# RWKV-like recurrence with an MLP mixer on one core: old state added on VectorE instead of TensorE from chunk 32 on, with a new order

## The chip, the cores and the metric

One core of a Trainium2 chip. The metric is the device time of one execution in microseconds, from several runs of each kernel; the median counts. Beside it stands one profiled execution, from which all rows of the trace come.

Engines: PE is TensorE (matmuls; its weight loads are a row of their own, PEld), DVE is VectorE, ACT is ScalarE, POOL is GpSimd, SP issues most of the DMAs. Each works through its own queue in order.

## What is computed

For each of 4 batch elements and 8 heads a state of 40 x 40 runs over 768 steps; its readings become the input of a token MLP and a channel MLP with residuals:

```
for t in range(S):                       # B=4, H=8, S=768, D=40
    y[:, :, t] = einsum('bhd,bhde->bhe', rt, state)
    Sa = einsum('bhde,bhe->bhd', state, at)
    state = state * wt[:, :, None, :] - einsum('bhd,bhe->bhde', Sa, bt) + einsum('bhd,bhe->bhde', vt, kt)
x = y as (B, S, 320)
u = x + (relu(x^T @ w_tok1) @ w_tok2)^T      # 768 -> 256 -> 768
out = u + relu(u @ w_ch1) @ w_ch2            # 320 -> 1536 -> 320
```

## The kernel before

The recurrence is done in chunks of 64 steps: 12 chunks for each batch element, 48 in all, numbered g. For each pair of chunks `t_a` and `t_b`/`t_b2` prepare matrices that don't depend on the state (cumulative products of w, products of k, b and a, and the inverse of a triangular matrix, which `t_solve` finds on VectorE for eight chunks at a time). `t_chain` then runs the chunks one behind the other, in two halves (`gi`) of four heads. One step `body(g)` of a half is:

- `pq` (L1165), a copy to the state buffer `Gb` on ScalarE (L1172), `pr2` (L1191): products with the old state; ScalarE negates the results into `W2s` (L1228, L1230), and the masks of L1200, L1216 and L1217 go on POOL and DVE (L1200 on whichever the planner finds free first)
- `pS` (L1250, L1252): the new state in PSUM. For two heads at a time, L1250 multiplies `kb` and `w2` into it, and L1252 adds the old state by a matmul with the identity `idS` as its stationary operand
- `sA`, `sB` (L1259, L1260): VectorE multiplies the sum by the chunk's decay `PC` into the other state buffer, odd heads first, then even ones. (Before chunk `gact` = 24 ScalarE does the even heads, L1263)
- `pU` (L307, called at L1270): the new state is transposed, and ScalarE copies it to `VSs` (L1280), which the next chunk's `pq` reads

The last chunk of a batch element (11, 23, 35, 47) leaves out everything from `pS` on. After each two chunks `t_y` (L1305, L1307) multiplies out the readings and `t_scale` (L1339) writes the MLP's input. `t_mlp` does the MLP of one batch element with matmuls of 320 and 384 columns (L1567, L1675); ScalarE and VectorE take turns to evict them (L1685, L1687, L1715). The MLP of one batch element runs beside the recurrence of the next ones; the last MLP stands alone at the end. `t_piece` (L397 to L1408) splits the MLP's weights early in the kernel.

The order on each engine is written out by a planner (class `Planner`, L77): each piece of work is a generator that yields operations with an estimated duration and has a rank; at each point the free engine takes the ready operation with the lowest rank. The numbers in `K` at the top are ranks, spans of ranks, assumed latencies and sizes of rings. `K` also steers dummy matmuls of 128 x 192 (L384, the fillers, written to a free part of `yb`): `fill` puts them where PE would idle and few columns went through PE lately (`fill_cols`), from `fill` thousand ns on; `behind` puts them ahead of ready work, too, until `pace_end` thousand ns, when the columns lag behind.

Of the kernel before, what the change touches and what calls it, by code (L numbers as in the profile page):

```python
# [14 lines left out]
ALU = mybir.AluOpType  # L15
# [7 lines left out]
def stepped(x, stride, n):  # L23
# [4 lines left out]
LAT = {"PE": 190.0, "ACT": 210.0, "DVE": 130.0, "POOL": 150.0, "SP": 40.0, "SWD": 100.0}  # L28


K = dict(lat=[133.111425, 147.657937, 109.14011, 163.056921], aff=2.209747, sets=[8, 8, 8, 8, 8, 8], atn=7, nab=2,
         nkp=2, nkb=3, npt=6, nw=3, mg=0.0, gv=-3.076, mc=286.785361, mv=0.0, gact=24, bp=24, eb=10, em=9,
         dml=1063.905408, dms=1.0, dme=100.0, pace=750.433365, pace_end=40.440937, ld=-5.808, pl=[-6.873], ptl=-3.864,
         pal=-1.426, kbl=-5.017, tbd_early=0, tbd=[["AD", "AD", "AD", "A"], ["AD", "AD", "AD", "A"]], alt_c=[1],
         slack=-10000.0, evm=6.119, slack_c=1397.683346, p_a=[0, 0, 0, 0], p_k=[0, 0, 0, 0], solve=[-0.397, -0.387569,
         5.786144, 2.822144, -1.128, -1.409856], solve_span=4.57, atomic=0, a=[9.899679, 10.839679, 10.739679,
         10.594962, 10.030679, 11.030962], a_span=[4.236, 5.059, 5.05, 6.316, 4.232, 5.642], b=0.938, chain=0.66,
         evac=10.486, y=1.793, utr=4.4, pem=2, mrg=1.171, ea=7, prp=15, w=3, c=2, m=2, fill=5.556509,
         fill_cols=3851.821616, mlp=[14.321, 27.212, 34.688, 50.415], mlp_span=[12.666389, 9.317, 10.305, 22.71],
         conv_t=8.117, conv_t_span=-4.601, conv_c=6.171, conv_c_span=13.011, conv_after=4)  # L40

# [237 lines left out]
def tile_kernel(ctx, tc, r, k, v, w, a, b, wt1, wt2, wc1, wc2, wT, aT, kbT, vT, rT, vt, out, dbg=None):  # L281
    nc = tc.nc
    B, H, S, D = r.shape
# [5 lines left out]
    DP, DQ = 104, 112  # L289
# [112 lines left out]
    tt = nc.vector.tensor_tensor  # L402
# [452 lines left out]
    def getG(g):  # L855
        return Gb[g % 2]

    def gS(x, e):
        return x[:, :, 64 + 64 * e:64 + 64 * e + D]
# [276 lines left out]
    def t_chain(gi):  # L1136
        h0 = gi * 4
        hs, p2 = slice(h0, h0 + 4), slice(gi * 2, gi * 2 + 2)
        def body(g):
            bi, c = divmod(g, NC)  # L1140
# [6 lines left out]
            kb, w2, hu, vs, rb = (o[n] for n in ("kb", "w2", "hu", "vs", "rb"))  # L1147
            G = getG(g)
# [6 lines left out]
            d = {}  # L1155


            prp = g >= K["prp"]

            def pcb(r0):  # L1160
                return PC[r0:r0 + D, g, p2].unsqueeze(2).to_broadcast([D, 2, D])
# [35 lines left out]
            hA, hB, lA, lB = slice(h0 + 1, h0 + 4, 2), slice(h0, h0 + 4, 2), slice(1, 4, 2), slice(0, 4, 2)  # L1197
            if prp:
# [6 lines left out]
                now = yield None  # L1205
                P.spawn(subv(), g - K["evac"], now)
                now = yield [pr2(j) for j in range(2)]
            else:
                now = yield [pr(j) for j in range(4)]
# [17 lines left out]
            if prp:  # L1227
                now = yield [("ACT", 245, lambda: nc.scalar.activation(out=w2[64:128, hA, 0:D], in_=d["pq"][64:128, :, DP:DP + D],  # L1228
                                                                       func=AF.Copy, scale=-1.0)),
                             ("ACT", 245, lambda: nc.scalar.activation(out=w2[64:128, hB, 0:D], in_=d["pq"][0:64, :, 64:DP],  # L1230
                                                                       func=AF.Copy, scale=-1.0))]
            else:
                now = yield [("ACT", 300, lambda: nc.scalar.activation(out=w2[64:128, hs, 0:D].rearrange("p (n e) c -> p n (e c)", e=2), in_=d["pq"][64:128, :, 64:144],
                                                                       func=AF.Copy, scale=-1.0))]
            P.set(w_ev, now)
            now = yield None
# [3 lines left out]
            if last:  # L1240
                P.set(chain_done[g][gi], now)
                return

            def pS(j):
                def f():
                    for z in range(2):
                        for h, q0 in ((h0 + 2 * j + 1, 64), (h0 + 2 * j, 0)):
                            dst = d["pS"][q0:q0 + D, h - h0, :]
                            if z == 0:
                                nc.tensor.matmul(dst, lhsT=kb[:, h, :], rhs=w2[:, h, 0:D], start=True, stop=False)  # L1250
                            else:
                                nc.tensor.matmul(dst, lhsT=idS[0:DP], rhs=gS(G, h % 2)[:, h // 2], start=False, stop=True)  # L1252
                return ("PE", (180, 320, "B"), f)
            d["pS"], tk = yield from bank("c", [128, 4, D], f"pS{g}_{gi}")
            yield [pS(j) for j in range(2)]
            if g >= 1:
# [2 lines left out]
            sA = ("DVE", 260, lambda: tt(out=gS(getG(g + 1)[64:DP, p2], 1), in0=d["pS"][64:DP, lA], in1=pcb(64), op=ALU.mult))  # L1259
            sB = ("DVE", 265, lambda: tt(out=gS(getG(g + 1)[64:DP, p2], 0), in0=d["pS"][0:D, lB], in1=pcb(0), op=ALU.mult))  # L1260

            def sc(j):
                return ("ACT", 205, lambda: nc.scalar.activation(out=gS(getG(g + 1)[64:DP, p2], 0)[:, j], in_=d["pS"][0:D, 2 * j],  # L1263
                                                                 func=AF.Copy, scale=PC[0:D, g, gi * 2 + j:gi * 2 + j + 1]))
            now = yield [sA, sc(0), sc(1)] if g < K["gact"] else [sA, sB]
            P.rel(tk, now)

            def pU(j):
# [15 lines left out]
        for g in range(NG):  # L1284
            yield from body(g)
# [622 lines left out]
```

## Time and profile before

| | us |
|---|---|
| median of 3 runs | 819.85 |
| the runs | 818.75 to 827.27 |
| the profiled execution | 826.04 |
| its span, first to last instruction | 824.2 |
| mean granted TensorE clock in it | 0.973 |

The times in the rows count from the start of the span. The durations of matmuls overlap, since they are pipelined: the busy time of a group is not what it costs the next. "Idle before" is the time an engine stood still ahead of an instruction, with what ended it behind the arrow. The granted clock is given as a share of full speed: 1.00 is 2.4 GHz, 0.50 is 1.2 GHz, and a value between is a mean over both.

### The profile page before, as it was taken

What the parts mean: (1) busy time and instruction counts of PE and PEld (TensorE: products, weight loads), DVE (VectorE), ACT (ScalarE), POOL (GpSimd) and SP (SyncE); (2) the same over time, 40 slices, a digit from 0 to 9 for tenths busy, and PEclk for the clock granted to TensorE, in tenths of its full rate; (3) what the DMA queues carried; (4) which work ended last, traced back from release to release, by engine and by line L of the source; (5) the groups of instructions that cost most, each with busy time, mean ns of one, the idle gap of its engine ahead of it and who ended that gap; (6) DMA issues with size and microseconds to landing.
All of it is one profiled execution on the core that took longest, in us unless ns stands there. A gap on an engine that the chain in (4) does not pass through costs nothing. (4 is left out here: it accounts for less than half of the span.)

```text
span 824.2 us, 27584 instructions
## 1 busy us (share of the span) xinstructions
PE 776.5 (94%) x11353; PEld 709.3 (86%) x11353; DVE 610.9 (74%) x1493; ACT 486.0 (59%) x1479; POOL 67.1 (8%) x143
## 2 busy tenths in 40 slices
PE   6797999888989989989999999999999999999997
PEld 6696888777878878879899899999999999998996
DVE  7999598998999878977879898499754433535342
ACT  5747887888778865765855746643654343443111
POOL 4000000000001110100101010001000010000000
PEclk9997897999999999989999999999999999999999
DMA  8964656778477975463677557244565534244341
GB/s 239 276 204 137 216 182 191 209 233 251 142 249 208 266 231 155 124 184 115 193 226 230 174 176 222 66 131 135 192 174 166 168 100 123 95 141 163 109 151 52
DMA packets 69077, 144.23 MB, mean 175 GB/s; under 512 B 8016, under 2 KB 45904, under 8 KB 65872
## 3 DMA queue, kind: packets, MB, share of 16 engines
q1 hardware_dynamic: 62608, 95.20, 39.1%
q0 software_dynamic: 6336, 47.19, 17.9%
q8 instruction: 92, 1.51, 0.8%
q14 instruction: 41, 0.34, 0.2%
HBM read 115.81 MB, written 26.54 MB: 173 GB/s over the span
## 5 line engine op out<-in xcount | busy, mean ns | idle before, releaser
L1675 PE MATMUL m<-ut,wg_c 128*128 128x384 f32 x768 | 162.5, 348 | 2.1 <-issue 2.0
L1567 PE MATMUL m<-wg_c,hd 128*128 128x320 f32 x864 | 157.3, 322 | 0.1
L1567 PEld LDWEIGHTS m<-wg_c,hd 128*128 128x128 f32 x864 | 131.3, 191 | 4.9 <-DVE hd L1687 2.2
L1675 PEld LDWEIGHTS m<-ut,wg_c 128*128 128x128 f32 x768 | 131.2, 189 | 2.2 <-DVE x L1715 0.5
L1685 ACT ACTIVATE hd<-m 128x384 fp32r<-128x384 f32 x96 | 47.2, 492 | 124.7 <-PE m L1675 118.1
L1687 DVE SCALAR_TENSOR_TENSOR hd<-m,hd 128x384 fp32r<-128x384 f32 x96 | 53.4, 556 | 57.9 <-ACT hd L1685 57.2
L1715 DVE TENSOR_TENSOR x<-m,x 128x320 f32<-128x320 f32 x96 | 46.8, 488 | 53.2 <-PE m L1567 52.5
L709 ACT ACTIVATE Dg<-px 128x128 f32<-128x128 f32 x144 | 56.5, 393 | 14.9 <-PE px L679 10.5
L1165 PE MATMUL pq<-RBs,VSs 104*104 104x128 f32 x384 | 57.8, 289 | 0.8 <-ACT VSs L1280 0.7
L1165 PEld LDWEIGHTS pq<-RBs,VSs 104*104 104x104 f32 x384 | 49.9, 180 | 3.2 <-ACT VSs L1280 1.5
L384 PE MATMUL yb<-ident 128*128 128x192 bf16 x479 | 46.3, 253 | 3.2 <-POOL ident masks.py:199 1.8
L1305 PE MATMUL yb<-KB,RM 128*64 128x40 f32 x768 | 47.3, 230 | 0.7 <-DVE RM L1222 0.7
L1307 PE MATMUL yb<-VSs,RBs 104*64 104x40 f32 x768 | 46.6, 229 | 0.0
L384 PEld LDWEIGHTS <-ident 128*128 128x128 bf16 x479 | 41.2, 101 | 4.9 <-issue 2.2
L1305 PEld LDWEIGHTS yb<-KB,RM 128*64 128x64 f32 x768 | 39.7, 137 | 4.9 <-issue 2.6
L1172 ACT COPY Gb<-pq 104x256 f32<-104x256 f32 x96 | 34.4, 373 | 15.1 <-PE pq L1165 13.6
L1307 PEld LDWEIGHTS yb<-VSs,RBs 104*64 104x64 f32 x768 | 39.7, 137 | 0.0
L397 DVE TENSOR_TENSOR cv_c<-cv_c 128x384 f32<-128x384 f32 (+3 forms) x72 | 36.5, 522 | 1.9 <-ACT cv_c L1408 1.5
L307 PE MATMUL pU<-ident,Gb 104*104 104x104 f32 x176 | 30.2, 268 | 8.0 <-DVE Gb L1259 3.5
L1200 POOL TENSOR_TENSOR RM<-Gb,upp 64x128 f32<-64x128 f32 x45 | 23.6, 531 | 169.2 <-ACT Gb L1172 169.0
L1250 PE MATMUL pS<-W2s,KB 128*40 128x40 f32 x704 | 33.6, 207 | 1.5 <-ACT W2s L1230 0.7
L307 PEld LDWEIGHTS pU<-ident,Gb 104*104 104x104 f32 x176 | 17.7, 132 | 19.1 <-ACT Gb L1263 6.5
(170 smaller groups left out, 1719.2 us busy)
## 6 DMA issues: line engine op xcount, KB each, us to landing
wg_c<-sG POOLq DMA_DIRECT2D x16, 1152.0 KB, 6.2
wg_c<-sG POOLq DMA_DIRECT2D x16, 960.0 KB, 5.4
KBp<-in_kbT_dram SPq DMA_DIRECT2D x24, 448.0 KB, 5.8
RBs<-in_rT_dram SPq DMA_DIRECT2D x48, 224.0 KB, 4.4
wg_t<-sT POOLq DMA_DIRECT2D x8, 1152.0 KB, 5.9
VSs<-in_vT_dram SPq DMA_DIRECT2D x48, 182.0 KB, 3.6
sKB<-KT SPq DMA_DIRECT2D x48, 160.0 KB, 3.1
KB<-sKB SPq DMA_DIRECT2D x48, 160.0 KB, 4.4
```

The source lines that it names most:

```text
L307: nc.tensor.matmul(out_, lhsT=in_, rhs=idn, start=True, stop=True, is_transpose=True)
L384: nc.tensor.matmul(yb[:, 320:512], lhsT=zf[:, 0:128], rhs=zf[:, 0:192], start=True, stop=True)
L397: return [(e, Port(60 + f * n / 0.96 if e == "DVE" else 140 + 2.24 * n), lambda e=e: engines[e].tensor_tensor(out=out_(), in0=a_(), in1=b_ ...
L709: return ("ACT", 190 if sl.start == 0 else 392, lambda: nc.scalar.activation(out=Dg[sl, :, ci * NP + h:(ci + 2) * NP:2].rearrange("p s n - ...
L1165: nc.tensor.matmul(stepped(d["pq"][0:DP, p, 0:64], 144, 2), lhsT=vs[:, gi * 2 + p, :], rhs=rb[:, gi * 2 + p, :].rearrange("p (h t) -> p h ...
L1305: nc.tensor.matmul(dst, lhsT=rms[g - 1 + z][:, h, :], rhs=o["kb"][:, h, :], start=True, stop=False)
L1307: nc.tensor.matmul(dst, lhsT=o["rb"][:, h // 2, q0:q0 + 64], rhs=o["vs"][:, h // 2, 64:DP], start=False, stop=True)
L1567: nc.tensor.matmul(d[key], lhsT=lhs(i, a_), rhs=rhs(i, b_), start=i == 0 and j == 0, stop=i == n - 1 and j == 2)
L1675: nc.tensor.matmul(pt, lhsT=mm_[q][0], rhs=mm_[q][1], start=q == 0, stop=q == len(mm_) - 1)
L1685: nc.scalar.activation(out=hid[key][:, 0], in_=pt, func=AF.Relu)
L1687: now = yield [("DVE", dve(TB_), lambda: nc.vector.scalar_tensor_tensor(out=hid[key][:, 1], in0=pt, scalar=0.0, in1=hid[key][:, 0].bitcast ...
L1715: now = yield [("DVE", dve(320), lambda: tt(out=x()[:, i], in0=d[("c2", g, i)], in1=x()[:, i], op=ALU.add))]
```

## The change

In `body(g)`, from chunk `ids` = 32 on, `pS` leaves out the matmuls with the identity, and VectorE adds the old state from `Gb` to the product, from PSUM into the new state's buffer. The multiplication by the decay then works in place on that buffer. The estimate for `pS` in the planner goes from 180 to 95 ns per pair of heads; the adds are entered with 245 ns and the multiplications with 220.

Besides this, most numbers in `K` are new: the ranks, the latencies that the planner assumes (POOL 109 to 60), `pace_end` 40.4 to 66.1, `fill` 5.56 to 7.33, `fill_cols` 3852 to 3950. The order of all engines' work thus changes in the whole kernel.

```diff
-K = dict(lat=[133.111425, 147.657937, 109.14011, 163.056921], ...
-         nkp=2, nkb=3, npt=6, nw=3, mg=0.0, gv=-3.076, mc=286.785361, mv=0.0, gact=24, bp=24, eb=10, em=9,
-         dml=1063.905408, dms=1.0, dme=100.0, pace=750.433365, pace_end=40.440937, ld=-5.808, pl=[-6.873], ptl=-3.864,
-         pal=-1.426, kbl=-5.017, ...
-         slack=-10000.0, evm=6.119, slack_c=1397.683346, ... solve=[-0.397, -0.387569,
-         5.786144, 2.822144, -1.128, -1.409856], solve_span=4.57, ...
-         utr=4.4, pem=2, mrg=1.171, ea=7, prp=15, w=3, c=2, m=2, fill=5.556509,
-         fill_cols=3851.821616, mlp=[14.321, 27.212, 34.688, 50.415], ...
+K = dict(lat=[134.375164, 147.383572, 60.325735, 170.500351], ...
+         nkp=2, nkb=3, npt=6, nw=3, mg=0.0, gv=-3.225, mc=286.180121, mv=0.0, gact=24, bp=24, ids=32, eb=10, em=9,
+         dml=1063.88097, dms=1.0, dme=100.0, pace=750.433365, pace_end=66.135854, ld=-6.411, pl=[-6.761], ptl=-3.957,
+         pal=-6.001, kbl=-10.216, ...
+         slack=-10000.0, evm=15.536, slack_c=1423.078504, ... solve=[-1.212, 0.322,
+         5.739, 2.822144, -1.255, 8.009], solve_span=4.472, ...
+         utr=2.73, pem=2, mrg=1.171, ea=7, prp=15, w=3, c=2, m=2, fill=7.332267, fill_cols=3950.0, mlp=[14.279,
+         27.102, 33.807, 50.292], ...
@@ body(g)
+            add = g >= K["ids"]
+
             def pS(j):
                 def f():
-                    for z in range(2):
+                    for z in range(1 if add else 2):
                         for h, q0 in ((h0 + 2 * j + 1, 64), (h0 + 2 * j, 0)):
                             dst = d["pS"][q0:q0 + D, h - h0, :]
                             if z == 0:
-                                nc.tensor.matmul(dst, lhsT=kb[:, h, :], rhs=w2[:, h, 0:D], start=True, stop=False)
+                                nc.tensor.matmul(dst, lhsT=kb[:, h, :], rhs=w2[:, h, 0:D], start=True, stop=add)
                             else:
                                 nc.tensor.matmul(dst, lhsT=idS[0:DP], rhs=gS(G, h % 2)[:, h // 2], start=False, stop=True)
-                return ("PE", (180, 320, "B"), f)
+                return ("PE", (95, 160, "B") if add else (180, 320, "B"), f)
...
-            now = yield [sA, sc(0), sc(1)] if g < K["gact"] else [sA, sB]
+            if add:
+                new = [gS(getG(g + 1)[64:DP, p2], e) for e in range(2)]
+                old = [gS(G[64:DP, p2], e) for e in range(2)]
+                yield [("DVE", 245, lambda: tt(out=new[1], in0=d["pS"][64:DP, lA], in1=old[1], op=ALU.add)),
+                       ("DVE", 245, lambda: tt(out=new[0], in0=d["pS"][0:D, lB], in1=old[0], op=ALU.add))]
+                sA = ("DVE", 220, lambda: tt(out=new[1], in0=new[1], in1=pcb(64), op=ALU.mult))
+                sB = ("DVE", 220, lambda: tt(out=new[0], in0=new[0], in1=pcb(0), op=ALU.mult))
+            now = yield [sA, sc(0), sc(1)] if g < K["gact"] and not add else [sA, sB]
```

## Rows read from the trace of the kernel before

**Rows 1.** The page: busy time of the engines, share of the span, instructions.
```profile
PE 776.5 (94%) x11353; PEld 709.3 (86%) x11353; DVE 610.9 (74%) x1493; ACT 486.0 (59%) x1479; POOL 67.1 (8%) x143
```
**Rows 2.** Busy by stretch: length; PE, PEld, DVE, ACT, POOL (instructions); clock, DMA share, GB/s.
```profile
0.00:329.70 329.70, 294.38 (x5641) 260.18 (x5645) 290.09 (x722) 245.73 (x771) 25.18 (x59) 0.95 0.71 212
329.70:495.00 165.30, 160.62 (x2211) 147.37 (x2203) 140.39 (x337) 104.44 (x321) 17.10 (x35) 0.97 0.58 178
495.00:742.00 247.00, 246.46 (x3039) 228.84 (x3038) 147.01 (x364) 118.59 (x346) 20.61 (x42) 1.00 0.47 142
```
**Rows 3.** Instructions of line L1252 from 494 to 745 us: ns min/median/max, first and last.
```profile
L1252 PE MATMUL pS<-Gb,ident x224: 200/202/208, 529.1 to 732.5; 104*40 104x40 f32 x112
```
**Rows 4.** Waits of PE, 495 to 742 us (one of two): us in total, times, longest.
```profile
PE pU L307 <- DVE Gb L1260: 0.2, 1, 0.2
```
**Rows 5.** Groups by line, 495 to 742 us: busy us, mean ns, idle before.
```profile
L1252 PE MATMUL pS<-Gb,ident 104*40 104x40 f32 x224 | 10.1, 202 | 0.0
L1200 POOL TENSOR_TENSOR RM<-Gb,upp 64x128 f32<-64x128 f32 x19 | 9.1, 481 | 57.1 <-ACT Gb L1172 56.9
```
**Rows 6.** Timeline of PE from 623.8 us: start, length, instruction.
```profile
623.91 0.25 PE L1250 MATMUL pS<-W2s,KB 128*40 128x40 f32 x4
...
624.45 0.25 PE L1252 MATMUL pS<-Gb,ident 104*40 104x40 f32 x4
624.63 1.66 PE L1675 MATMUL m<-ut,wg_c 128*128 128x384 f32 x8
626.13 0.34 PE L307 MATMUL pU<-ident,Gb 104*104 104x104 f32 x2
626.24 1.64 PE L1675 MATMUL m<-ut,wg_c 128*128 128x384 f32 x8
```
**Rows 7.** Instructions on tile pS from 494 to 745 us, VectorE's.
```profile
L1260 DVE TENSOR_TENSOR Gb<-pS,PC x30: 233/234/236, 493.9 to 733.0; 40x80 f32<-40x80 f32 x30
L1259 DVE TENSOR_TENSOR Gb<-pS,PC x29: 244/245/247, 494.2 to 732.7; 40x80 f32<-40x80 f32 x29
```
**Rows 8.** Lines L1200 and L1217 in the whole span.
```profile
L1200 POOL TENSOR_TENSOR RM<-Gb,upp x45: 446/454/1169, 258.4 to 724.7; 64x128 f32<-64x128 f32 x45
L1200 DVE TENSOR_TENSOR RM<-Gb,upp x21: 275/284/435, 259.1 to 735.4; 64x128 f32<-64x128 f32 x21
L1217 DVE TENSOR_TENSOR RM<-pq,upp x66: 283/284/288, 261.6 to 737.0; 64x128 f32<-64x128 f32 x66
```
**Rows 9.** Busy time by stretch, VectorE alone (busy, instructions), and the sum of 540 to 590.
```profile
570.00:580.00 10.00, 9.62 (x21) 1.00 0.67 205
...
sum 50.00, DVE 45.13; mean DVE 9.03
```
**Rows 10.** Busy time by stretch of line L1252 alone, PE and PEld (instructions).
```profile
540.00:550.00 10.00, 0.71 (x16) 0.60 (x16) 1.00 0.77 221
...
580.00:590.00 10.00, 0.51 (x16) 0.39 (x12) 1.00 0.63 212
```
**Rows 11.** Busy time by stretch, PE alone, where the fillers stand.
```profile
51.20:54.61 3.41, 3.41 (x44) 1.00 0.41 122
```
**Rows 12.** Busy time by stretch of line L384, the fillers: PE and PEld.
```profile
0.00:41.20 41.20, 15.68 (x145) 13.48 (x145) 1.00 0.93 257
41.20:64.80 23.60, 20.84 (x251) 20.71 (x252) 1.00 0.64 190
...
sum 824.20, PE 46.30 PEld 41.15; mean PE 11.57 PEld 10.29
```
**Rows 13.** Busy time by stretch, PE alone (busy, instructions, granted clock), at half clock.
```profile
71.70:88.70 17.00, 13.72 (x275) 0.52 0.59 172
126.30:136.50 10.20, 10.18 (x158) 0.53 0.77 232
```
**Rows 14.** Timeline of PE ahead of the first fall of the clock.
```profile
69.64 0.63 PE L971 MATMUL pe<-DT,N 32*32 32x32 f32 x16 [1.14 <-DVE DT L935]
71.71 0.49 PE L924 MATMUL pm<-ET,TBn 32*32 32x32 f32 x20 [1.45 <-ACT ET L931]
```

More of the change, by code (lines that the diff above doesn't have):

```diff
@@ L28 @@
 LAT = {"PE": 190.0, "ACT": 210.0, "DVE": 130.0, "POOL": 150.0, "SP": 40.0, "SWD": 100.0}
-K = dict(lat=[133.111425, 147.657937, 109.14011, 163.056921], aff=2.209747, sets=[8, 8, 8, 8, 8, 8], atn=7, nab=2,
-         nkp=2, nkb=3, npt=6, nw=3, mg=0.0, gv=-3.076, mc=286.785361, mv=0.0, gact=24, bp=24, eb=10, em=9,
-         dml=1063.905408, dms=1.0, dme=100.0, pace=750.433365, pace_end=40.440937, ld=-5.808, pl=[-6.873], ptl=-3.864,
[L34 to L40, printed above, removed]
+K = dict(lat=[134.375164, 147.383572, 60.325735, 170.500351], aff=2.209747, sets=[8, 8, 8, 8, 8, 8], atn=7, nab=2,
+         nkp=2, nkb=3, npt=6, nw=3, mg=0.0, gv=-3.225, mc=286.180121, mv=0.0, gact=24, bp=24, ids=32, eb=10, em=9,
+         dml=1063.88097, dms=1.0, dme=100.0, pace=750.433365, pace_end=66.135854, ld=-6.411, pl=[-6.761], ptl=-3.957,
+         pal=-6.001, kbl=-10.216, tbd_early=0, tbd=[["AD", "AD", "AD", "A"], ["AD", "AD", "AD", "A"]], alt_c=[1],
+         slack=-10000.0, evm=15.536, slack_c=1423.078504, p_a=[0, 0, 0, 0], p_k=[0, 0, 0, 0], solve=[-1.212, 0.322,
+         5.739, 2.822144, -1.255, 8.009], solve_span=4.472, atomic=0, a=[11.407, 10.839679, 10.739679, 10.594962,
+         9.839, 12.16], a_span=[4.236, 5.059, 5.05, 5.669, 4.232, 7.635], b=0.938, chain=0.651, evac=9.595, y=1.774,
+         utr=2.73, pem=2, mrg=1.171, ea=7, prp=15, w=3, c=2, m=2, fill=7.332267, fill_cols=3950.0, mlp=[14.279,
+         27.102, 33.807, 50.292], mlp_span=[12.798665, 9.733, 12.449, 22.732665], conv_t=7.405, conv_t_span=-4.188,
+         conv_c=6.183, conv_c_span=12.951, conv_after=4)
 class Port(float):
```

## The prediction

> **What bounds the kernel now.** I read the page's busy shares first, then the four long stretches of the span, then the changed instructions in the stretch where they stand, and last the rows that price a delay.
>
> The page has TensorE (PE) busy for 94% of the span, VectorE (DVE) 74% [rows 1]. Such a share is a mean over stages with different limits, so the stretches come next [rows 2]. From 0 to 329.7 us PE is busy 294.4 of 329.7 us at a mean granted clock of 0.95, and DVE nearly as long, 290.1 us: no single engine rules there, and time goes into idle stretches, into dummy matmuls (fillers), and into half clock. From 329.7 to 495 us PE idles 4.7 us at clock 0.97. From 495 to 742 us PE is busy 246.46 of 247 us at clock 1.00, with DVE at 147.0 us (60%) and ScalarE (ACT) at 118.6 us (48%). There PE is the bound. From 742 us on the last MLP runs alone, PE again.
>
> Where do the edited instructions stand? The identity matmuls of L1252 run all over the recurrence. A matmul of this type is recorded as two instructions, so a chunk with 8 heads gives 16. The chunks that the edit touches are 32 to 46 without 35 and 47 (the last chunk of a batch element does no update): 3 + 11 = 14 chunks, 14 x 16 = 224 instructions. Counted back from the end, these are exactly the 224 from 529.1 to 732.4 us [rows 3]. So all that the edit takes off PE lies in the stretch where PE is the bound, at full clock. PE's waits in this stretch that the trace can name are two of 0.2 us, both ahead of pU [rows 4].
>
> **The change, part by part.**
>
> *Removed: 112 matmuls (224 instructions) on PE.* Their summed busy time is 10.1 us at 202 ns each [rows 5], but they overlap: in the chunk at 623.9 us, L1250 and L1252 take turns, and their groups of four, eight of them, start at even distances: from the first at 623.91 to the eighth at 624.45 us are seven steps, so 0.077 us each [rows 6]. Such a group is one product for two heads. A chunk has four groups of L1252, so it gives back 4 x 0.077 = 0.31 us, and 14 chunks give **4.3 us**. The bounds: nothing, if the holes aren't closed, and 10.1 us, if each counted at its full duration. I take the pitch between starts, since with a PE that never stops it is what the next matmul gains.
>
> *Added: 56 VectorE instructions.* Per half chunk, two adds (product in PSUM plus old state in SBUF) stand ahead of the two multiplications, which now read and write SBUF. An add has the form of L1259/L1260, 40 x 80 with one operand from PSUM: 245 and 234 ns [rows 7]. Whether an operand comes from SBUF rather than PSUM made no difference in the one pair of rows that allows a comparison: the mask of L1200 reads SBUF only, that of L1217 reads PSUM, both 64 x 128, both 284 ns at the median [rows 8]. So I keep 240 ns for all four instructions; the low end is the 234 ns of L1260, the high end the 435 ns that the longest L1200 on DVE took. Four more instructions a chunk are 4 x 0.24 = 0.96 us, and 14 chunks are 13.4 us (13.1 to 24.4 us). DVE in the bound stretch goes from 147 to about 160 of 247 us. Most of the cost is therefore covered: the 247 us of PE work run beside it. Without that cover it would be the third rival below.
>
> The tightest place is 540 to 590 us, where DVE also solves for the last set: it is busy 45.13 of 50 us, and 9.62 of 10 us from 570 us on [rows 9], so it idles 4.87 us. Three of the touched chunks have their product there, 16 instructions each [rows 10], so 2.9 us of the 4.87 are used up. It fits, but narrowly; what is queued behind the adds on DVE is the MLP's evictions (L1687, L1715), and PE waits for those only when both of its MLP banks are full.
>
> One rule of the skill speaks against the multiplications. The rows first: on GpSimd (POOL) L1200 takes 454 ns at the median and up to 1169 ns, on DVE 284 and up to 435 ns [rows 8], and in the bound stretch POOL does 19 of them [rows 5]. The Trainium skill, page "SBUF — State Buffer", section "Who interferes with whom", says that a VectorE instruction with two SBUF inputs and a GpSimd instruction that reads SBUF exclude each other for their full length. The long L1200 rows would fit that. Today's multiplications have one input in PSUM; the new ones have both in SBUF. By chance meetings, 56 x 19 x (0.24 + 0.48) / 247 gives 3 collisions at up to 0.48 us, 1.5 us in all, on engines that aren't the bound. By the rule the sum would lose 1.5 us only if each collision reached PE; by the rows of PE's waits it loses nothing. I take nothing.
>
> *Longer: the step of the recurrence.* Product, two adds, two multiplications, transposition pU: both halves share DVE, so pU of the second half comes up to 0.96 us later per chunk. What hides it is MLP work: in the chunk at 624 us, eight matmuls of 1.66 us run before the first pU and eight more before the second [rows 6]. The PSUM bank of pS is held two instructions (0.5 us) longer.
>
> *The order searched anew.* Every rank in K moves, mostly by little; the scheduler's release latency for POOL drops from 109 to 60, the filler rule that runs even ahead of ready work is on until 66 instead of 40 us, fillers may start at 7.3 instead of 5.6 us, and their threshold rises from 3852 to 3950 columns. All are costed at nothing in the sum, and this is the term I know least. The longer filler rule has little room: between 51 and 58 us PE is already full of fillers, 44 in 3.41 us, busy 3.41 us [rows 11]. Of the 46.3 us of PE's time that are fillers, 15.68 + 20.84 = 36.5 us stand before 64.8 us [rows 12]. What a new order can win or lose lies in the idle and half-clock time of the first 330 us.
>
> *The sum.* The profiled execution took 826.04 us: a span of 824.2 and 1.84 us around it. Less 4.3 us it would be 821.7 us. The median of the runs is 819.85 us, 6.2 us below the profiled one. The saving lies in a stretch without idle time and at full clock, so I carry it over whole: 819.85 - 4.3 = **815.5 us**.
>
> **The rivals.**
>
> *The new order wins early time too.* The clock falls to half in several places, the two longest at 0.52 granted over 17 us from 71.7 us and 0.53 over 10.2 us from 126.3 us [rows 13]. Ahead of the first, PE waited for VectorE's DT and ScalarE's ET [rows 14]. If this PE work had run at full clock, it would have taken 13.72 x 0.48 + 10.18 x 0.47 = 11.4 us less. An order that spares half of it gives 815.5 - 5.7 = 809.8 us. For it: fillers are allowed a little more freely now. Against it: no edit is aimed at the waits that start the dips, and DVE is as busy there as before.
>
> *The saving doesn't come through.* PE's queue is in order; if the new order puts waits where the removed matmuls were, or the last MLP starts no earlier because its input waits for DVE, the 4.3 us become idle time: 819.85 us. For it: DVE's 90% between 540 and 590 us [rows 9] and its in-order queue. Against it: 0.4 us of waits today.
>
> *The VectorE chain becomes the bound (slower).* If PE has no ready work behind pS, each chunk's additional 0.96 us shows in full: 14 x 0.96 = 13.4 us, 819.85 - 4.3 + 13.4 = 829.0 us. It breaks even where PE has about 0.65 us too little ready work a chunk (0.31 won against 0.96 lost). For it: the adds are in series with the recurrence, and both halves share one queue. Against it: chunks are some 14.5 us apart (14 of them in 203 us), and a step can slip by 1 us while MLP matmuls remain; they last until after the last chunk.
>
> **How the numbers follow.** PE-bound and the saving comes through, give or take 2.5 us of order: 0.50, 813 to 818 us. Early time won too: 0.20, 804 to 813. Saving lost: 0.18, 818 to 823. Chain bound: 0.12, 823 to 830. The forecast is the first. The range of 807 to 823 us leaves out about half of the second and most of the last, some 0.2. One per cent of 819.85 is 8.2 us, about what a measurement of this kernel can tell from no change: faster means below 811.7, slower above 828. Faster: most of the second case and a little of the first, 0.20. Slower: the upper half of the last, 0.07. Within: 0.73.
>
> **What would show it.** Right: L1252's successor has 224 instructions fewer, the stretch from the first changed chunk to the last has PE busy without gaps at clock 1.00, and it is about 4 us shorter; DVE has 56 more instructions of 230 to 245 ns and some 13 us more busy time; POOL's and DVE's L1200 stay near 454 and 284 ns. Wrong in the size of the order's term: the first 330 us have become longer or shorter by more than the late stretch; the dips of the clock have moved. Wrong in the cover: PE's waits name the two added lines or pU behind them, or MLP matmuls wait for L1687 and L1715 in 540 to 590 us.

## The result, and the profile after

The changed kernel takes 828.22 us (median of 22 runs, 820.71 to 833.56), the kernel before 821.25 us beside it (22 runs). The ratio of the runs is 1.0074 with a 95% interval of 1.0048 to 1.0100: slower by 0.7%, within the 1% of "no change", but above the range of 807 to 823 us and on the other side of the forecast of 815.5 us. Here and below, ratios and the mean clocks beside them are taken from the fast runs, those within 1.5% of the fastest of the same kernel. The profiled execution has a span of 826.1 us at a mean granted clock of 0.962 (before: 824.2 and 0.973).

Busy by stretch after, in the columns of [rows 2]; the stretches are those of before:

```profile
0.00:329.70 329.70, 294.92 (x5544) 260.25 (x5545) 281.51 (x699) 244.43 (x761) 23.02 (x56) 0.91 0.71 205
329.70:495.00 165.30, 162.98 (x2185) 149.53 (x2185) 149.77 (x357) 108.70 (x332) 17.19 (x37) 1.00 0.62 195
495.00:742.00 247.00, 245.76 (x2907) 225.09 (x2904) 158.81 (x428) 117.88 (x344) 20.74 (x41) 1.00 0.44 137
```

PE is still the bound from 495 to 742 us, at full clock. The first 330 us have the same busy PE time as before (294.9 and 294.4 us), but at a clock of 0.91 instead of 0.95.

Instructions on tile pS from 494 to 780 us (ns min/median/max, first and last start), which answer to [rows 3] and [rows 7]. L1252 is now the product, L1254 the identity; L1270 and L1271 are the adds:

```profile
L1252 PE MATMUL pS<-W2s,KB x240: 200/207/231, 499.1 to 726.1; 128*40 128x40 f32 x120
L1270 DVE TENSOR_TENSOR Gb<-pS,Gb x28: 244/245/246, 515.9 to 727.0; 40x80 f32<-40x80 f32 x28
L1271 DVE TENSOR_TENSOR Gb<-pS,Gb x28: 233/234/236, 516.2 to 727.3; 40x80 f32<-40x80 f32 x28
L1254 PE MATMUL pS<-Gb,ident x16: 200/202/203, 499.2 to 499.7; 104*40 104x40 f32 x16
```

The 16 identity matmuls left belong to the last untouched chunk. The lines of the two multiplications, which now read SBUF alone:

```profile
L1272 DVE TENSOR_TENSOR Gb<-Gb,PC x28: 228/232/242, 516.9 to 727.8; 40x80 f32<-40x80 f32 x28
L1273 DVE TENSOR_TENSOR Gb<-Gb,PC x28: 234/235/237, 517.2 to 728.1; 40x80 f32<-40x80 f32 x28
```

The waits of PE from chunk 32's first pS (514.9 us) to the end, in the columns of [rows 4]:

```profile
PE m L1576 <- DMA wg_t<-sT: 1.3, 1, 1.3
PE pU L307 <- DVE Gb L1273: 0.5, 3, 0.2
PE pU L307 <- DVE Gb L1272: 0.2, 1, 0.2
```

The masks of L1200, in the columns of [rows 8], keep their medians of 454 and 284 ns:

```profile
L1200 POOL TENSOR_TENSOR RM<-Gb,upp x43: 444/454/1503, 268.4 to 723.0; 64x128 f32<-64x128 f32 x43
L1200 DVE TENSOR_TENSOR RM<-Gb,upp x23: 258/284/486, 268.3 to 731.4; 64x128 f32<-64x128 f32 x23
```

So the edit is made as described, its instructions last as long as estimated, and PE hardly waits behind it. The time must have gone elsewhere.

### The profile page after: what moved, and what is told of

It reads as the page before. It is cut to its first block, busy times and chain, and to the rows that moved or that the text cites. A ratio compares the mean times of both kernels' runs of the same rounds, so it can differ in the third digit from the quotient of the medians.

```text
span 826.1 us, 27163 instructions
## 1 busy us (share of the span) xinstructions
PE 780.1 (94%) x11115; PEld 709.3 (86%) x11115; DVE 623.1 (75%) x1552; ACT 487.8 (59%) x1478; POOL 65.2 (8%) x141
## 4 chain that ended last, share of the span: by engine, by line
PE 66%; DVE 12%; ACT 9%; issue 7%; DMA 4%; POOL 1%; SPq 0%; POOLq 0%; ACTq 0%; DVEq 0%
PE m L1576 17%; PE m L1684 15%; PE pq L1165 5%; PE pq L1191 3%; ACT Dg L709 2%; PE px L679 2%; PE yb L1314 2%; PE pU L307 2%; PE pq L1186 2%; PE ph L1103 2%; PE yb L1316 2%; PE pk L307 2%; PE ph L1015 1%; PE pt L1084 1%; DMA wg_c<-sG 1%
## 5 line engine op out<-in xcount | busy, mean ns | idle before, releaser
L1576 PE MATMUL m<-wg_c,hd 128*128 128x320 f32 x864 | 154.5, 319 | 0.0
L1576 PEld LDWEIGHTS m<-wg_c,hd 128*128 128x128 f32 x864 | 129.2, 188 | 5.1 <-DVE hd L1696 1.5
L1314 PE MATMUL yb<-KB,RM 128*64 128x40 f32 x768 | 49.6, 234 | 1.4 <-issue 0.8
L1316 PE MATMUL yb<-VSs,RBs 104*64 104x40 f32 x768 | 48.3, 232 | 0.0
L384 PE MATMUL yb<-ident 128*128 128x192 bf16 x465 | 46.0, 257 | 0.0
L384 PEld LDWEIGHTS <-ident 128*128 128x128 bf16 x465 | 40.6, 102 | 1.7 <-issue 0.5
L1200 POOL TENSOR_TENSOR RM<-Gb,upp 64x128 f32<-64x128 f32 x43 | 21.8, 515 | 184.8 <-ACT Gb L1172 166.8
L1510 POOL DMA_DIRECT2D wg_c<-sG x32 | 18.1, 567 | 184.2 <-PE m L1684 85.0
L1252 PE MATMUL pS<-W2s,KB 128*40 128x40 f32 x704 | 31.4, 208 | 1.3 <-ACT KT L620 0.6
```

The costliest lines, as they stand in the source:

```text
L384: nc.tensor.matmul(yb[:, 320:512], lhsT=zf[:, 0:128], rhs=zf[:, 0:192], start=True, stop=True)
L1314: nc.tensor.matmul(dst, lhsT=rms[g - 1 + z][:, h, :], rhs=o["kb"][:, h, :], start=True, stop=False)
L1316: nc.tensor.matmul(dst, lhsT=o["rb"][:, h // 2, q0:q0 + 64], rhs=o["vs"][:, h // 2, 64:DP], start=False, stop=True)
L1576: nc.tensor.matmul(d[key], lhsT=lhs(i, a_), rhs=rhs(i, b_), start=i == 0 and j == 0, stop=i == n - 1 and j == 2)
```

## The experiments

Two things changed at once: the edit in `body(g)`, and the order that the planner writes from the new `K`. The experiments take them apart. Beside the ratio I use one number from the trace: the time from chunk 32's first pS to the end of the span, where nearly everything runs at full clock and which leaves out the first 500 us with their changing clock. It compares only kernels with the same numbers in `K`, since the new order leaves more MLP work behind chunk 32. Two executions of one kernel agree in it within 0.4 us while the clock in it stays up (295.17 and 295.18 us before, 311.20 and 310.82 us in the changed kernel).

**The yardstick.** The kernel before once more.

> The kernel before, unchanged, as a reference on the same chip and for a second profile. Both theories: ratio 1.00. Theory A (the loss is half-clock time of the new order in the first 330 us): here the mean granted clock over 0 to 330 us is 0.95 or more, against 0.91 in the changed kernel. Theory B (the loss is the edit itself, by VectorE's longer chain): the clock over the first 330 us tells nothing, and the stretch from chunk 32 on is faster here than with the edit.

Measured: 1.0019 [0.9982, 1.0056], span 822.9 us, clock 0.971. From chunk 32's first pS on (columns of [rows 2]):

```profile
527.72:822.90 295.18, 287.43 (x3148) 270.10 (x3147) 156.06 (x387) 114.87 (x330) 23.42 (x46) 1.00 0.43 136
```

PE is busy 287.43 of 295.18 us, idle 7.75. The execution of the prediction gives 295.17 us as well (529.03 to 824.2).

**The edit in the old order, the order in the old kernel.**

```diff
# edit, old order: the K of before, and
+         ids=32
# new order, no edit: the new K, and
-         ids=32
+         ids=48
```

> The edit alone: all numbers of K as before, ids=32 added. PE's order is that of before up to the first matmul that falls out in chunk 32; from there the planner goes on with the new estimates. Theory A: the edit is worth its 4.3 us, ratio 0.995 (816 to 818 us where before has 821), the first 330 us as before. Theory B: the edit costs, ratio 1.004 to 1.010 (824 to 829 us), with PE waiting on the added VectorE lines from chunk 32 on. A third outcome, 1.00: the saving turns into idle time or fillers.

> The new order alone: all numbers of K as in the changed kernel, but ids=48, so that every chunk keeps the products with the identity. PE's order is that of the changed kernel up to chunk 32. Theory A: slower than the changed kernel by the 4.3 us of the edit, ratio 1.0074 + 0.005 = 1.012 to 1.013 (831 us), with the mean clock over 0 to 330 us near 0.91. Theory B: the new order costs nothing, ratio 1.00 (821 us).

> The changed kernel, unchanged, as the fourth corner on the same chip. Both theories: ratio 1.005 to 1.010. If the effects of edit and order add, its ratio is that of the edit alone times that of the order alone.

Measured: edit with the old numbers 1.0138 [1.0081, 1.0196]; new order without the edit 1.0128 [1.0075, 1.0181]; the changed kernel beside them 1.0101 [1.0056, 1.0146]. By these medians each half alone costs more than both together, though the intervals overlap; the costs of edit and order do not add, which would give 1.027. The new order alone costs 0.0128 x 822 = 10.5 us (6 to 15). From chunk 32 on, first the changed kernel, then the new order without the edit:

```profile
514.90:826.10 311.20, 302.26 (x3083) 281.38 (x3082) 174.65 (x463) 123.25 (x351) 22.70 (x44) 1.00 0.43 134
518.12:830.40 312.28, 305.08 (x3307) 285.59 (x3306) 161.80 (x403) 123.56 (x351) 24.39 (x48) 1.00 0.42 134
```

The changed kernel needs 311.20 and 310.82 us in two executions, the new order without the edit 312.28 us: with the new numbers the edit wins 1.1 to 1.5 us, not 4.3.

With the old numbers the planner knows of the adds and moves other work between pS and pU, so the order after chunk 32 changes. That stretch takes 301.34 us, 6.2 more than before:

```profile
522.76:824.10 301.34, 291.51 (x2941) 268.89 (x2940) 168.27 (x447) 113.98 (x329) 22.04 (x43) 1.00 0.42 133
```

PE's busy time goes up, to 291.51 us, though 224 of the recurrence's instructions are gone. Two things in the trace go with that: 31 fillers stand in the stretch instead of 14 (3.23 us instead of 1.33), and TensorE changes between operand sizes more often, 142 times instead of 104 with rows and columns rounded up to 32, 64 or 128. What each costs was not tried.

**The edit alone, in a fixed order.** To keep the order, the planner is given for the touched chunks the operations and estimates of before, and issues two VectorE instructions where it planned one. PE lacks the 112 matmuls, VectorE has the 56 adds; the queues of ACT and POOL are, instruction by instruction in the traces, those of the old order.

```diff
-                return ("PE", (95, 160, "B") if add else (180, 320, "B"), f)
+                return ("PE", (180, 320, "B"), f)
...
-                yield [("DVE", 245, <add odd>), ("DVE", 245, <add even>)]
-                sA = ("DVE", 220, <multiply odd>)
-                sB = ("DVE", 220, <multiply even>)
+                sA = ("DVE", 260, <add odd, add even>)
+                sB = ("DVE", 265, <multiply odd, multiply even>)
```

> The edit in the order of before: the planner keeps its old estimates, each of its two VectorE entries now issues two instructions (both adds, then both multiplications). The order of ScalarE, GpSimd and the DMAs is that of before; TensorE lacks 112 products with the identity, VectorE has 56 adds more, and nothing else moves. Theory A (the edit saves its 4.3 us, and what the edit alone with the old numbers lost came from the order that the planner made of the rest): from chunk 32's product to the end 295.2 - 4.3 = 290.9 us, ratio 0.995. Theory B (the longer VectorE chain itself holds PE up): 297 to 301 us, ratio 1.002 to 1.010, PE waiting for the added lines. In between: 292 to 295 us, a part of the saving lost to waits.

> The same in the order of the new numbers without the edit: ScalarE, GpSimd and DMAs as in the new order alone, TensorE without the 112 products, VectorE with 56 adds. From chunk 32's product to the end that kernel took 312.3 us. Theory A: 308.0 us, ratio 1.0128 - 0.005 = 1.007 to 1.008. Theory B: 311 us or more, ratio 1.010 to 1.015.

Measured: old order 1.0147 [1.0103, 1.0192], a repetition 1.012 [1.0062, 1.0178]; new order 1.0198 [1.0157, 1.0238]. From chunk 32 on, the old order with the edit:

```profile
520.15:822.40 302.25, 285.76 (x2924) 265.68 (x2923) 167.26 (x443) 114.92 (x330) 23.39 (x46) 1.00 0.43 133
```

7.1 us more than before, with PE less busy and idle 16.49 us instead of 7.75. The ratio stands for some 12 us (8 to 16); part of the rest goes with the lower clock of these runs, 0.971 against 0.975 before. The largest wait of PE in that stretch:

```profile
PE pU L307 <- DVE Gb L1277: 7.1, 15, 0.7
```

In the fixed new order, the stretch and the wait:

```profile
517.71:840.90 323.19, 306.15 (x3083) 284.51 (x3082) 173.25 (x459) 124.00 (x351) 24.50 (x48) 0.99 0.40 129
PE pU L307 <- DVE Gb L1277: 9.3, 18, 0.8
```

That is 10.9 us more than the 312.28 us without the edit, some 4 us of it by falls of the clock inside the stretch. So in either order the edit costs when the plan doesn't know of it; with the new numbers a plan that knows of it wins a little, with the old ones it loses.

Where does the wait come from? One step of the kernel before (timeline, PE and VectorE; start, length):

```profile
714.98 0.25 PE L1252 MATMUL pS<-Gb,ident 104*40 104x40 f32 x4
715.15 0.70 PE L1567 MATMUL m<-wg_c,hd 128*128 128x320 f32 x3
715.20 0.24 DVE L1259 TENSOR_TENSOR Gb<-pS,PC 40x80 f32<-40x80 f32 x1
715.46 0.23 DVE L1260 TENSOR_TENSOR Gb<-pS,PC 40x80 f32<-40x80 f32 x1
...
715.84 0.36 PE L307 MATMUL pU<-ident,Gb 104*104 104x104 f32 x2
```

The same step with the edit in the old order (L1276 and L1277 are the multiplications):

```profile
712.50 0.48 PE L1252 MATMUL pS<-W2s,KB 128*40 128x40 f32 x16
712.91 0.70 PE L1581 MATMUL m<-wg_c,hd 128*128 128x320 f32 x3
713.27 0.24 DVE L1272 TENSOR_TENSOR Gb<-pS,Gb 40x80 f32<-40x80 f32 x1
713.54 0.23 DVE L1273 TENSOR_TENSOR Gb<-pS,Gb 40x80 f32<-40x80 f32 x1
713.70 0.23 DVE L1276 TENSOR_TENSOR Gb<-Gb,PC 40x80 f32<-40x80 f32 x1
713.96 0.23 DVE L1277 TENSOR_TENSOR Gb<-Gb,PC 40x80 f32<-40x80 f32 x1
...
714.35 0.36 PE L307 MATMUL pU<-ident,Gb 104*104 104x104 f32 x2 [0.73 <-DVE Gb L1277]
...
715.31 0.36 PE L307 MATMUL pU<-ident,Gb 104*104 104x104 f32 x2 [0.29 <-DVE Gb L1277]
```

Before, two multiplications end at 715.69 and PE comes out of three MLP matmuls at 715.84: the old order gives pU just enough cover. With the edit PE gets there earlier, since pS is shorter, and VectorE later, by two more instructions. PE stands 0.73 + 0.29 us, more than the 0.31 us that pS gave back.

**One half of the edit at a time**, both in the fixed old order: the identity products dropped with no adds (the old state is then left out from chunk 32 on), and the adds made with the products kept (the old state is then added twice).

```diff
# drop only: no adds, sA and sB as before
+                    for z in range(1 if add else 2):
# adds only: the products stay
+                    for z in range(2):
```

> TensorE's half of the edit alone, in the order of before: from chunk 32 on the products with the identity are left out and nothing takes their place, so the old state is missing from the sum. The order of every engine is that of before. Theory: the removal is worth what the pitch gave, 14 x 0.30 = 4.2 us: from chunk 32's product to the end 291 us against 295.2, ratio 0.995. Rival: the gaps aren't closed (PE's order stays, and waits for other work set the pace): 294 to 295 us, ratio 0.999 to 1.000.

> VectorE's half of the edit alone, in the order of before: from chunk 32 on the 56 adds are made and the products with the identity are kept too, so that the old state is counted twice. Theory: the adds cost what was lost in the fixed order: 302.25 - 291 = 11 us; from chunk 32's product to the end about 306 us, ratio 1.017 to 1.020, PE waiting at pU for the second multiplication. Rival: without the removal PE reaches pU later by 0.3 us a chunk, so that half of the wait is covered: 300 to 303 us, ratio 1.010 to 1.014.

Measured: drop only 0.9994 [0.9950, 1.0038], adds only 1.0087 [1.0043, 1.0130]. From chunk 32 on, drop only:

```profile
526.70:820.60 293.90, 283.72 (x2924) 265.79 (x2923) 155.96 (x387) 114.71 (x330) 23.39 (x46) 0.99 0.44 137
```

and adds only:

```profile
535.53:838.30 302.77, 289.84 (x3148) 269.89 (x3147) 167.29 (x443) 115.27 (x330) 23.47 (x46) 1.00 0.43 133
```

Dropping the products takes 3.7 us off PE's busy time (287.43 to 283.72), but 2.4 us of it turn into idle time, and 1.3 us are left: PE now reaches pU before VectorE is done even with the short chain (four waits):

```profile
PE pU L307 <- DVE Gb L1262: 2.5, 4, 1.6
```

The adds cost 7.6 us. Of these, 5.2 us are more idle time of PE (4.9 us of waits at pU), and 2.4 us are more busy time with the same matmuls, whose cause no run shows. Together -1.3 + 7.6 = 6.3 us, against 7.1 for both at once: they add, nearly, from one execution each.

**pU later in PE's queue.** If the price is only PE standing at pU, it must fall when pU moves behind MLP matmuls that stood after it. In the fixed old order each pU from chunk 32 on, with its copy, is held until TensorE has been given up to 1.2 us of other work. The queues of VectorE, ScalarE and GpSimd stay as they were. A new use of its PSUM bank ends the hold early, so many pU move less.

```diff
+        if getattr(fn, "late", False):       # pU and its copy
+            self.held = self.held + [(fn, op[6])]
+            return
...
+        if self.held and op[3] == "PE":
+            self.left_ -= ns
+            if self.left_ <= 0.0:
+                self.flush()
```

> The edit in the fixed old order (as e5), but each pU from chunk 32 on, with its copy, is issued up to 1.2 us of TensorE's work later in TensorE's queue, behind MLP matmuls that were behind it; all other queues are unchanged. Theory A (the price of the adds is TensorE standing at pU because pU's place in its in-order queue was chosen for the shorter VectorE chain): the waits of PE at pU on VectorE (7.1 us in e5) fall by at least half, and from chunk 32's first pS to the end of the span it takes 296 to 299 us instead of 302.25; ratio 1.005 to 1.012 beside 1.0147. Theory B (the adds cost by themselves, through VectorE's load or its evictions, wherever pU stands): waits turn up elsewhere (next pq on the copy, MLP evictions), the stretch stays within 1 us of 302, ratio as e5.

> The edit in the fixed old order once more, on the same chip as the kernel with pU later. Both theories: ratio 1.010 to 1.019, waits of PE at pU on VectorE about 7 us, 302 us from chunk 32's first pS to the end.

Measured: 1.0074 [1.0026, 1.0122], beside 1.0120 for the same kernel without the hold. The stretch from chunk 32 on and the wait:

```profile
530.32:830.20 299.88, 286.60 (x2924) 266.16 (x2923) 166.76 (x443) 115.51 (x330) 23.45 (x46) 1.00 0.43 134
```

```profile
PE pU L325 <- DVE Gb L1297: 3.8, 10, 0.6
```

299.9 us, against 302.25 and 305.13 us in the two executions without the hold, and the wait falls to 3.8 us from 7.1 and 8.5. The 305.13 us have a fall of the clock in them (0.89 from 552 to 567 us), so 302.25 is the one to compare with: 2.4 of the 7.1 us come back. The kernel with fillers at the end of this section repeats it, at 300.06 us. The intervals of the ratios overlap, the rows do not. This lies just short of theory A (at least half of the wait, 299 us at most) and outside theory B. So a third of the loss is shown to follow pU's place; the rest is not, since ten pU still wait.

**The clock of the new order.** The new order's cost should be early: from chunk 32 on it runs at full clock, with PE idle 7.20 us (312.28 - 305.08), no more than before. Busy by stretch in the kernel before (the yardstick run):

```profile
0.00:150.00 150.00, 129.46 (x2472) 115.12 (x2472) 130.28 (x325) 106.12 (x318) 11.88 (x34) 0.91 0.69 206
150.00:250.00 100.00, 90.44 (x2014) 79.13 (x2015) 90.33 (x232) 78.79 (x248) 2.13 (x6) 0.93 0.69 207
```

In the new order without the edit:

```profile
0.00:150.00 150.00, 128.36 (x2300) 113.49 (x2301) 125.66 (x313) 100.16 (x298) 11.88 (x33) 0.86 0.67 196
150.00:250.00 100.00, 93.31 (x2044) 82.06 (x2043) 86.16 (x226) 79.77 (x249) 2.35 (x7) 0.90 0.70 206
```

In the changed kernel, with one of its falls of the clock:

```profile
0.00:150.00 150.00, 127.18 (x2368) 112.53 (x2369) 128.06 (x320) 102.05 (x301) 11.91 (x33) 0.89 0.67 196
150.00:250.00 100.00, 92.76 (x2021) 81.78 (x2018) 85.56 (x224) 78.13 (x245) 2.35 (x7) 0.86 0.72 207
...
160.00:164.00 4.00, 2.14 (x62) 1.00 0.98 318
164.00:187.00 23.00, 22.33 (x398) 0.55 0.66 186
```

From 160 to 164 us PE is busy 2.14 of 4 us, as it waits for VectorE's AT, and the next 23 us run at 0.55, near the lower level of 1.2 GHz. Over the whole span, what the clock takes from PE is at most (1 - 0.971) x 822.9 = 23.9 us before, (1 - 0.960) x 830.4 = 33.2 us in the new order without the edit, and (1 - 0.962) x 826.1 = 31.4 us in the changed kernel; the time at half clock is twice that, and not all of it is busy. The 9.3 us between the first two are about the size of the order's 10.5 us. The means over the runs say the same: 0.975 before (92 runs), 0.961 with the new order (6), 0.965 with new order and edit (26).

The runs can also be sorted by their own mean clock, which differs from one execution to the next of the same kernel:

| mean clock of an execution | before: executions, mean us | changed: executions, mean us |
|---|---|---|
| 0.954 to 0.959 | none | 4, 831.1 |
| 0.960 to 0.964 | none | 11, 829.3 |
| 0.965 to 0.969 | 12, 824.6 | 3, 825.6 |
| 0.970 to 0.974 | 23, 822.9 | 7, 824.0 |
| 0.975 to 0.979 | 40, 820.5 | 1, 820.7 |
| 0.980 to 0.985 | 17, 816.7 | none |

At one clock the two kernels differ by about 1 us or less; the changed kernel runs more often at a low one. A straight line through the executions of before gives 5.6 us for 0.010 of clock. Extended below the clocks that before reached, an estimate, it gives the new order without the edit (830.7 us on the mean at 0.961, before 820.9 at 0.975) some 8 of its 10 us, and the changed kernel (827.4 us at 0.965) nearly 6 of its 6.5. Clock and time go together here, which isn't a proof: a wait that makes an execution longer could also be what lowers its clock.

That the clock is the cause was then tried by giving TensorE more dummy matmuls in gaps that the planner sees, with no instruction of another engine moved.

```diff
+            if e == "PE" and self.filler is not None and t0 < 250e3:
+                gap = t0 - max(self.free["PE"], self.filler[0], self.hold)
+                for _ in range(int(0.6 * gap / 80.0) if gap > 160.0 else 0):
+                    self.filler[3]()
# dense: t0 < 330e3, 1.0 * gap / 80.0, gap > 80.0
```

> The changed kernel with 103 more fillers in the first 250 us, in gaps where the planner has PE idle, and without the planner's knowing: the order of all other work is that of the changed kernel, instruction by instruction. If half-clock time is what the new order costs, the mean clock over the first 330 us rises from 0.91 to 0.95 or more, and the time falls by 4 to 9 us, ratio 0.999 to 1.005. If the clock's dips lie under waits for VectorE anyway, the clock rises and the time stays at ratio 1.007 to 1.010. If fillers delay real work, slower.

> The edit in the order of before with 126 more fillers in the first 250 us, placed in the same way. If both the edit's saving and the clock's are real: ratio 0.985 to 0.992 (808 to 814 us), the fastest of all. If only the edit's is: 0.995. If the fillers delay real work: above 0.995.

> The kernel before with 126 more fillers in the first 250 us, in gaps where the planner has PE idle, the order of all other work unchanged. If the clock sets the first 330 us: mean clock of the whole run from 0.974 to 0.98 or more, as the same fillers did beside the edit in the fixed order (0.969 to 0.980, 833.0 to 826.7 us on the mean), ratio 0.992 to 0.996, faster than both kernels. If the fillers only take the place of waits: 0.998 to 1.003.

> The changed kernel with 206 more fillers in the first 330 us, twice as many as in the last try, in every planned gap of over 80 ns; all other work in the same order. If the half-clock time of the new order is what makes it slower, the mean clock goes from 0.964 to 0.975 or more and the time to ratio 0.997 to 1.003. If the new order's loss lies elsewhere, the clock rises and the time doesn't fall. If the clock doesn't rise, the dips come from work of few columns and not from gaps, and fillers in gaps can't mend them: ratio 1.006 to 1.010.

| kernel | fillers added | mean clock of the same runs | ratio to before |
|---|---|---|---|
| changed | 0 | 0.965 | 1.0074 [1.0048, 1.0100] |
| changed | 103 | 0.972 | 1.0030 [0.9993, 1.0068] |
| changed, dense | 206 | 0.975 | 1.0055 [1.0015, 1.0096] |
| edit, fixed old order | 0 | 0.971 | 1.0147 [1.0103, 1.0192] |
| edit, fixed old order | 126 | 0.980 | 1.0064 [1.0033, 1.0095] |
| before | 0 | 0.975 | 1.0019 [0.9982, 1.0056] |
| before | 126 | 0.980 | 1.0014 [0.9978, 1.0051] |

In the old order 126 fillers raise the clock by 0.009 and win back 0.8% of the edit's kernel; on the kernel before they raise it by 0.005 and win nothing that the interval shows. In the changed kernel 103 fillers have an unclear effect: the clock is 0.972 in the seven runs that the ratio is taken from, but 0.964 over all twelve, with a median of 827.8 us. 206 fillers lift the clock to the level of before, yet the median only falls from 828.2 to 825.2 us, and the intervals of the two ratios overlap. At the line's 5.6 us for 0.010 of clock more would have come back, so the fillers seem to cost part of it themselves. That the clock is most of the order's 10 us is thus supported from two sides, but not shown.

**Filler numbers or ranks?** The changed kernel with the `pace_end`, `fill` and `fill_cols` of before, and the other way round the best mixture for the edit: old order, pU later, 126 fillers.

```diff
-  pace_end=66.135854, fill=7.332267, fill_cols=3950.0
+  pace_end=40.440937, fill=5.556509, fill_cols=3851.821616
```

> The changed kernel with the four-number filler rule of before (pace_end 40.4, fill 5.56, fill_cols 3852), all other new numbers kept; the order changes with it, 563 fillers instead of 465. Theory A (the filler numbers of the new K cost the clock): mean granted clock back to 0.970 or more, ratio below 1.002. Theory B (it is the ranks: where the early work stands): clock stays at 0.96 to 0.967 and the ratio at 1.005 to 1.015.

> The edit in the fixed old order with pU later, and with 126 more fillers in the planned gaps of the first 250 us, as in e8. If what the adds cost and what the clock costs are separate and add: e8's 1.0064 less what pU's later place gives back (3 to 6 us, 0.4 to 0.7%), so 0.999 to 1.003, clock about 0.98. If the adds cost wherever pU stands: 1.006 as e8.

Measured: 1.0386 [1.0329, 1.0443] at a mean clock of 0.953, worse than either theory said. With the new ranks, going back to the old filler numbers costs some 3%, so the new filler numbers by themselves are not what makes the changed kernel slower; the plan of every engine changes with them, though, and by the line above the lower clock is only some 7 of these 27 us. What is left for the cost are the ranks, latencies and spans, and which of them was not tried. The mixture: 1.0016 [0.9979, 1.0053], 0.5% below the 1.0064 without the hold, at a mean clock of 0.981. From chunk 32 on:

```profile
523.14:823.20 300.06, 286.65 (x2924) 266.24 (x2923) 166.69 (x443) 115.33 (x330) 23.42 (x46) 1.00 0.43 134
```

That is still 4.9 us more than before. So the mixture is as fast as the kernel before, but it does not undo the edit's loss: by the line above, the higher mean clock (0.981, against 0.974 of the kernel before beside it) makes up for some 4 us.

## Why the prediction was wrong, step by step

**PE as the bound, and the saving.** Right in the place and in the price: PE is busy 245.76 of 247 us at full clock, and a whole chunk's pS before MLP resumes takes 0.41 us (712.50 to 712.91 in the timeline above) against 0.72 us in [rows 6] (623.91 to 624.63), so the 0.31 us a chunk that I had. What failed is "I carry it over whole": with the products dropped alone, PE's busy time fell by 3.7 us, but PE's queue is in order, and the next instruction that needs VectorE wasn't ready sooner. 1.3 us came through with no adds at all. The bound "nothing, if the holes aren't closed" was nearer than the 4.3 us I took.

**56 VectorE instructions.** Right: 245, 234, 232 and 235 ns, and VectorE is busy 623.1 us instead of 610.9. That 13 us of work fit beside PE's 247 us was right too, and beside the point: the price was not VectorE's share but the length of the chain.

**The tight place from 540 to 590 us.** Not what hurt. After, VectorE is busy 43.98 of those 50 us, and the 15 waits in the fixed old order are spread over the touched chunks; those in the timeline above stand at 714 and 715 us, and from 700 to 730 us VectorE is busy 13.75 of 30 us. Next to it, though, one wait comes from VectorE's queue and not from a thin cover: at 597 us PE stands 0.51 us behind 5.11 us of MLP work, because the adds stand behind L1353, which by the trace itself waits 4.91 us for that work.

**The port.** The Trainium skill, page "SBUF — State Buffer", section "Who interferes with whom", says that a VectorE instruction with two SBUF inputs contends with a GpSimd instruction that reads SBUF, for ports under an exclusive lock. One meeting here agrees in kind. In 13 executions of kernels with the new multiplications, 56 in each, a single one ran at the same time as an L1200 on POOL, in the edit with the old numbers:

```profile
729.41 0.45 POOL L1200 TENSOR_TENSOR RM<-Gb,upp 64x128 f32<-64x128 f32 x1 [3.90 <-ACT Gb L1172]
729.63 0.34 DVE L1272 TENSOR_TENSOR Gb<-Gb,PC 40x80 f32<-40x80 f32 x1
```

It took 335 ns, where all others took 228 to 242. It was held up by 0.1 us, less than the 0.2 us that L1200 still had to run when it started, so the two did not exclude each other for their full length. Such meetings are also rarer than my chance count of 3 in each execution: in the changed kernel there were none. Nothing was the right value.

**pU later, hidden by MLP work.** This is the step that failed for the edit. I read the cover from one chunk, that of [rows 6], where 1.66 us of MLP work stand ahead of the first pU and as much ahead of the second. In the old order that is a roomy one. In the trace of the yardstick run, 14 of the 28 pU of the touched chunks (one for each half) have at most 1.4 us of other matmuls between their pS and themselves; the timeline above shows such a step, with three matmuls of 0.70 us, then two of 0.54. VectorE's additional instructions don't fit in there, and with the edit 15 waits stand at pU. The third rival named the mechanism and its break-even (0.65 us a chunk too little), and in the old order it decides: 7.1 us net, where its full price was 13.4 - 4.3 = 9.1 us. That the place in PE's queue is the cause was tried with pU later, and a third of the loss came back. Its argument against, that chunks are 14.5 us apart, counted the slack of the recurrence, not that of PE's queue.

**The new order at nothing.** The step that failed for the sum. Without the edit the new order costs 10.5 us (6 to 15). With the adds in its plan it gives pU its cover: PE's waits at pU are 9.3 us where the new numbers plan without the adds, and 0.7 us in the changed kernel. And it pays in the first 250 us with a lower clock, which by the estimate above goes with some 8 of the 10 us. I had looked there only for a gain (the first rival, from the dips of [rows 13] and [rows 14]) and gave no chance to a loss from the same place. I also gave the longer filler rule "little room"; without the new filler numbers the new ranks run at 0.953 instead of 0.965 and lose 27 us more.

**The sum as measured:** the order +10.5 us, the edit within it -1.1 to -1.5 us, so about +9; the runs of the changed kernel say +6 and +8 us (1.0074 and 1.0101), within the intervals. That 828 us lies next to the third rival's 829.0 us is chance: in the changed kernel PE waits 0.7 us for VectorE's chain.

**What stays open:** which ranks place the early work so that the clock falls, whether the clock causes the 8 us that go with it, what the other 4.7 us of the edit's loss in the old order are, and whether some order keeps both the early clock of before and the cover for pU. The mixture above came to par, no further.

## What to carry to other kernels

Work taken off the busiest engine is only won if the next instruction in its in-order queue is ready earlier (here 1.3 of 4.3 us); count that cover for every repetition of the step, at its tightest, not in one roomy example. A longer chain on an engine with spare time still costs, as soon as it is longer than the work that the waiting engine has between giving and taking. When an edit comes with a newly searched order, run the order without the edit and the edit without the order before pricing either; here each lost by itself. And sort the executions by their own clock before explaining a difference between kernels.

## What the runs showed of the hardware

The same work in another order, with 465 dummy matmuls instead of 479, ran at a mean granted clock of 0.961 (6 runs) instead of 0.975 (92 runs). Between executions of the kernel before, 0.010 of mean clock went with 5.6 us. Dummy matmuls are no free cure: 206 of them raised the clock of the changed kernel by 0.010, and its median fell by 3 us, within the intervals. In VectorE's chain the third instruction, which reads what the first wrote, started 0.16 us after the second, which lasts 0.23 us, while the second came 0.27 us after the first: the four took 0.92 us from 713.27 us to the last one's end. The one multiplication with both inputs in SBUF that met a GpSimd instruction reading SBUF took 335 ns instead of 228 to 242.
